# A convolution with generated weights and a two-branch maxout layer: columns taken in rotated order, a start with casting transfers, and row copies moved to VectorE

## The chip, the core and the metric

The kernel runs on one core of one Trainium2 chip. The metric is the device time of one execution in microseconds (us), the median of the runs. The core has a matrix engine (TensorE, PE in the profile; its loading of weights is PEld), VectorE (DVE), ScalarE (ACT), GpSimd (POOL) and SyncE (SP), and 16 DMA engines that move data between memory (DRAM) and the on-chip buffer (SBUF). SP and POOL are here above all issuers of transfers. A transfer that POOL issues may change the number format on its way (a casting transfer, f32 in DRAM to bf16 in SBUF); those that SP issues here copy as they are.

## The reference

x has 8 batches of 4160 rows of 192 numbers. Each row is replaced by a weighted sum of itself and its six predecessors in the same batch (zeros ahead of the first), with weights from a softmax over 7 taps for each of 8 heads of 24 numbers. The result y goes through h1 = y @ w1, h2 = y @ w2, g = max(h1, h2), out = g @ w_out:

```python
w = np.exp(weight_gen - max); w = w / (w.sum(-1) + 1e-09)      # 7 taps, 8 heads
x_pad = np.concatenate([zeros(B, 6, D), x], axis=1)
y[b, s, h] = sum over k of w[b, s, h, k] * x_pad[b, s + k, h]   # 24 numbers a head
g = np.maximum(y @ w1, y @ w2)                                  # (33280, 1024)
out = g @ w_out                                                 # (33280, 192)
```

The kernel uses max(h1, h2) = h1 + relu(h2 - h1): it computes y @ (w2 - w1), takes relu of it, and adds y @ (w1 @ w_out) in the second product.

## The kernel before, in words

The 33280 rows lie as 128 partitions of 260 columns: partition p holds rows 260p to 260p + 259, so 16 partitions make one batch of x. A column is one row of x in each partition. **Batches** (line 50) are runs of 16 columns for the softmax, 17 of them, the last of 4 columns. **Units** (line 63) are the pieces of a batch that VectorE turns into y: 4 columns in batches 0 and 1, 8 columns in the others, and the last batch is one unit of 4. **Tiles** (line 68) are pieces of hidden rows, 260 in all, one per column on average; **groups** (line 71) are two, later three, tiles.

For one unit, VectorE multiplies x by the weights (mul, L182, one instruction for all 7 taps) and adds the taps up (adds, L198, L204, L207). The result is turned round: by SP's DMA transpose (L216) from unit 8 on, by TensorE against an identity (sum_transpose, L248, with the adding done there too) and a ScalarE copy (L255) in units 0 to 7. TensorE then forms the hidden tile (hid_tile, L299), ScalarE takes its relu (L309), and TensorE adds the columns of the output (L351, L339), which ScalarE copies (L395) and SP stores (L409). For a batch's weights, ScalarE takes an exponential (exp_sum, L135), VectorE sums it (red, L147), ScalarE takes the logarithm (ln, L151), VectorE subtracts it (shift, L156), and ScalarE takes the exponential of that (weights, L167). The next loads are issued on POOL after an instruction `gate` that waits for a transpose's landing (L224).

Everything is issued in program order on each engine; there is no scheduler. The order after the start is given by `extra(t)` (line 758: which mul and adds go beside which tile) and by due times in `due` (line 731) for ScalarE's softmax steps. `behind(first, load)` makes a transfer wait until `first` is done.

**The start** (lines 520 to 695). SP issues, one behind another: the softmax input of batch 0 (wg_t); the six columns before column 0, the halo, which are the last six of the partition above (xs, L523, in two transfers); columns 0 to 3 (L532); the first halves of w1 and w2, rows 0 to 127 (ws0E, ws1E, L541); their rows 128 to 191, in four transfers (ws0T, ws1T, L549); columns 4 to 7; the second halves of w1 and w2 (L541 again); and the softmax input of batch 1. All of it is f32. In partitions that begin a batch the halo must be zero: a mask (L557 to L561) multiplies it (L568 on VectorE, L570 on ScalarE), while L574 and L620 cast columns 0 to 3 and 4 to 7 to bf16. VectorE's order is: softmax of batch 0, casts, mul of unit 0, `w_diff(0)` (the difference of the first halves L584 and of the last rows L589), cast L620, mul of unit 1, `w_diff(1)`, red of batch 1, mul of unit 2. The copies of difference rows to other partitions (L586, L587, L591) are on ScalarE in `w_diff(0)` and on VectorE in `w_diff(1)`. ScalarE casts w1 to bf16 (L580, L633, L634), which w1_transposed (L603) needs. TensorE's first matmuls are only there to keep it busy (keep_warm, L615): 30 ahead of the first sum_transpose and 8 behind it. Hidden tiles 0 and 1 use the first halves of the difference, 2 and 3 the second.

**The end.** The last batch is the unit of 4 columns; TensorE's last work is the output of the last 8 columns (rest_of_results, line 489).

## Time and profile before

| | |
|---|---|
| time, median of 3 runs (lowest, highest) | 410.28 us (409.76, 410.6) |
| span of the profiled execution | 408.8 us |
| between the span and the median | 1.5 us |
| busy: PE, DVE, ACT, POOL | 399.1, 373.4, 357.2, 75.5 us |
| first mul, first hidden tile start | 9.12, 15.47 us |
| last y on DVE ends, last hidden tile starts | 379.30, 397.22 us |
| last matmul ends | 404.98 us |

The trace gives the profiled execution's span, from its first to its last instruction; a time of that one execution with what lies around the span is not given, so the 1.5 us stand between its span and the median of the runs. A row of the timeline has the start, the duration, the engine, the line, the operation with what it writes and reads, the shape, the number of such instructions, and in brackets how long the engine was idle before it and what ended that. Durations of queued instructions overlap a little. "POOLq" and "SPq" rows are issues of transfers; the transfers land some us later.

### The profile page before, as it was taken

To read this page: it belongs to the slowest core of one execution; us is meant where nothing else is said; L and a number is where in the kernel's file an instruction comes from. 1 tells how busy PE (TensorE), PEld (TensorE's weight loads), DVE (VectorE), ACT (ScalarE), POOL (GpSimd) and SP (SyncE) were. 2 spreads that over 40 slices of the span, in tenths; PEclk is the share of its full clock that TensorE was granted. 3 is DMA by queue.
4 is the path that set the end of the run, shared out by engine and by line. 5 is a ranking of instruction groups with operands and counts; after the bars stand their busy time and mean duration, and the time that the engine had idled before them with its cause. 6 is when DMAs were issued, how large, how long until landed. Compare 5 with 4: busy or idle time off the path is not lost.

```text
span 408.8 us, 16064 instructions
## 1 busy us (share of the span) xinstructions
PE 399.1 (98%) x7386; PEld 317.5 (78%) x7386; DVE 373.4 (91%) x217; ACT 357.2 (87%) x424; POOL 75.5 (18%) x101
## 2 busy tenths in 40 slices
PE   7899999999999999999999999999999999999996
PEld 2688999777777877778777777877787776787796
DVE  5999999999999999999999999999999999999100
ACT  6799999999899998999998999998999888988872
POOL 0311011222221022221111222220121221210000
PEclk9999999999999999999999999999999999999999
DMA  8958477667647854965785397478649638643704
GB/s 240 229 118 217 126 148 164 159 150 182 148 102 198 226 129 98 260 167 85 214 231 117 91 256 186 74 243 168 146 98 250 169 59 223 177 88 108 187 35 161
DMA packets 60784, 65.68 MB, mean 161 GB/s; under 512 B 47631, under 2 KB 49039, under 8 KB 60718
## 3 DMA queue, kind: packets, MB, share of 16 engines
q1 hardware_dynamic: 52334, 40.54, 35.6%
q0 software_dynamic: 8240, 24.04, 29.5%
q8 instruction: 57, 0.93, 0.9%
q10 hardware_dynamic: 144, 0.10, 0.1%
q14 instruction: 9, 0.07, 0.1%
HBM read 35.96 MB, written 25.56 MB: 150 GB/s over the span
## 4 chain that ended last, share of the span: by engine, by line
PE 78%; DVE 7%; ACT 7%; DMA 5%; issue 1%; SPq 1%; DVEq 0%; ACTq 0%
PE op_ps L339 36%; PE hd L299 33%; PE op_ps L351 7%; ACT rd_t L309 4%; DVE m_t L182 4%; DMA ws1T<-in_moe_w_dram 2%; DMA out_dram<-o_t 1%; PE hdp L299 1%; PE yps L248 1%; DVE m_t L204 1%; DVE m_t L198 1%; DMA yt<-y_t 1%; ACT en_t L167 1%; ACT o_t L395 1%; DVE y_t L207 0%
## 5 line engine op out<-in xcount | busy, mean ns | idle before, releaser
L309 ACT ACTIVATE rd_t<-hd 128x1024 bf16<-128x1024 f32 (+1 forms) x206 | 234.4, 1188 | 27.8 <-PE hd L299 26.6
L339 PE MATMUL op_ps<-wo,rd_t 64*128 64x192 bf16 x4160 | 211.4, 243 | 0.4 <-issue 0.3
L339 PEld LDWEIGHTS <-rd_t 64*128 64x128 bf16 x4160 | 181.5, 94 | 16.2 <-issue 0.5
L299 PE MATMUL hd<-yt,wd 64*128 64x512 bf16 (+1 forms) x1584 | 187.8, 360 | 0.9 <-DMA yt<-y_t 0.7
L182 DVE TENSOR_TENSOR m_t<-xb_t,en_t 128x10752 bf16<-128x10752 bf16 (+1 forms) x37 | 187.4, 5070 | 0.2
L299 PEld LDWEIGHTS <-wd 64*128 64x128 bf16 x1776 | 94.8, 94 | 42.4 <-issue 2.0
L224 POOL CAST gate<-yt 128x1 f32<-128x1 bf16 x29 | 41.0, 1415 | 264.6 <-DMA yt<-y_t 264.6
L198 DVE TENSOR_TENSOR m_t<-m_t 128x4608 bf16<-128x4608 bf16 (+1 forms) x31 | 75.5, 2434 | 0.1
L395 ACT COPY o_t<-op_ps 128x384 f32<-128x384 f32 (+1 forms) x99 | 57.1, 588 | 13.4 <-PE op_ps L339 13.4
L351 PE MATMUL op_ps<-w,yt 64*128 64x192 bf16 x780 | 55.9, 243 | 0.2 <-ACT o_t L395 0.2
L351 PEld LDWEIGHTS <-yt 64*128 64x128 bf16 x780 | 38.5, 94 | 16.5 <-issue 1.3
L204 DVE TENSOR_TENSOR m_t<-m_t 128x3072 bf16<-128x3072 bf16 (+1 forms) x29 | 50.0, 1723 | 0.1
L167 ACT ACTIVATE en_t<-wg_t 128x896 bf16<-128x896 f32 (+2 forms) x45 | 35.6, 817 | 0.0
L207 DVE TENSOR_TENSOR y_t<-m_t 128x1536 bf16<-128x1536 bf16 (+1 forms) x29 | 27.3, 941 | 0.5
L114 POOL DMA_DIRECT2D xb_t<-in_x_dram x33 | 17.6, 534 | 29.9 <-ACT rd_t L309 18.9
L156 DVE TENSOR_TENSOR wg_t<-wg_t,sum_t 128x280 f32<-128x280 f32 (+5 forms) x46 | 22.0, 480 | 0.0
L147 DVE TENSOR_REDUCE sum_t<-e_t 128x64 f32<-128x448 f32 (+2 forms) x31 | 19.6, 635 | 2.6 <-ACT e_t L135 2.5
L135 ACT ACTIVATE e_t<-wg_t 128x896 f32<-128x896 f32 (+2 forms) x18 | 16.1, 901 | 2.5 <-DMA wg_t<-in_weight_gen_dram 2.5
L309 ACT ACTIVATE rd_t<-hdp 128x1024 bf16<-128x1024 f32 x16 | 16.2, 1031 | 0.6 <-PE hdp L299 0.4
L615 PE MATMUL warm<-ident 128*128 128x512 bf16 x38 | 11.5, 474 | 2.6 <-DVE ident L562 2.6
L299 PE MATMUL hdp<-yt,wd 64*128 64x256 bf16 x192 | 13.5, 270 | 0.3 <-issue 0.2
L248 PE MATMUL yps<-ident,m_t 64*128 64x64 bf16 x600 | 10.5, 191 | 1.5 <-DVE m_t L182 1.5
(45 smaller groups left out, 65.0 us busy)
## 6 DMA issues: line engine op xcount, KB each, us to landing
out_dram<-o_t SPq DMA_DIRECT2D x27, 768.0 KB, 4.9
xb_t<-in_x_dram POOLq DMA_DIRECT2D x30, 384.0 KB, 5.1
wg_t<-in_weight_gen_dram POOLq DMA_DIRECT2D x14, 448.0 KB, 5.4
xb_t<-xb_t POOLq DMA_DIRECT2D x16, 288.0 KB, 5.2
out_dram<-o_t SPq DMA_DIRECT2D x10, 384.0 KB, 3.3
wg_t<-in_weight_gen_dram SPq DMA_DIRECT2D x2, 448.0 KB, 4.5
xs<-in_x_dram SPq DMA_DIRECT2D x2, 384.0 KB, 6.7
xb_t<-in_x_dram POOLq DMA_DIRECT2D x3, 192.0 KB, 5.0
```

Of the source, the lines that this page charges most:

```text
L156: nc.vector.tensor_tensor(out=w_t, in0=w_t, in1=_sub(s_ts[b], hs.start, [[1, hs.stop - hs.start], [0, K]]), op=ALU.subtract)
L167: nc.scalar.activation(out=_sub(en_ts[b], (o * WGC + j * N * K) * 2, [[2 * N, K], [2, N], [1, 2]]), in_=_sub(wg_ts[b], (o * H + j * N) * K ...
L182: return nc.vector.tensor_tensor(out=m_out, in0=x_in, in1=_sub(en_ts[b], o * WGC * 2, [[2, K * n * H], [0, G // 2], [1, 2]]), op=ALU.mult,)
L198: nc.vector.tensor_tensor(out=taps(0, 1, 3), in0=taps(0, 1, 3), in1=taps(3, 1, 3), op=ALU.add)
L204: nc.vector.tensor_tensor(out=taps(0, 2, 2), in0=taps(0, 2, 2), in1=taps(1, 5, 2), op=ALU.add)
L207: nc.vector.tensor_tensor(out=_sub(y_ts[b], o * D, [[64, 2], [P, 3 * w // 2], [1, 64]]), in0=taps(0, 1, 1), in1=taps(2, 1, 1), op=ALU.add,)
L224: nc.gpsimd.tensor_copy(out=gate, in_=yt[:, 0:1])
L299: nc.tensor.matmul(hid_out(t, f, j), lhsT=wd_at(j, s, f // 4, f % 4 * P, P), rhs=_sub(yt_ts[u][half(j), :], (s + j) % 3 * P, [[3 * P, w // ...
L309: relu_of[t0] = nc.scalar.activation(out=rd[:, k * 1024:(k + n) * 1024], in_=hd[:, at:at + n * 1024], func=AF.Relu)
L339: return nc.tensor.matmul(op_out(c), lhsT=rd[half(r), k * 1024 + at:k * 1024 + at + P], rhs=wo[half(r), f * D:(f + 1) * D], start=False, s ...
L351: nc.tensor.matmul(op_out(c + j), lhsT=yt_ts[u][half(j), (3 * i + (s + j) % 3) * P:(3 * i + (s + j) % 3 + 1) * P], rhs=w10[half(j), s * D: ...
L395: nc.scalar.copy(out=_sub(o, c % 24 * D, [[D, len(qs)], [h * D, 2], [1, D]]), in_=_sub(tile_, at + (qs[0] - p) * D, [[D, len(qs)], [512, 2 ...
```

## The change

Columns are taken in an order rotated by 8: the kernel's column c is column (c + 8) mod 260 of the partition. The first batch is then columns 8 to 23, whose six predecessors are in the same partition, and the last batch is columns 0 to 7, whose halo is the end of the partition above. Batch 15 has 12 columns (units of 8 and 4), batch 16 has 8 (two units of 4).

At the start one casting transfer on POOL brings halo and first four columns of batch 0, ten columns; the mask and the four casts are gone, the halo of the last batch comes from DRAM with zeros copied over the partitions that begin a batch. SP's transfers of the weights wait for the first exponential. The last rows of w1 and w2 are issued half on SP, half on POOL. The second half of w1 comes a second time as a casting transfer, so L634 is gone. All copies of difference rows are on VectorE, and `w_diff(1)` stands ahead of the mul of unit 1. There are 19 and 5 matmuls of keep_warm. Hidden tile 2 and w1_transposed stand ahead of the sum_transpose of unit 1.

```diff
-    BATCHES = [(c, min(16, CPP - c)) for c in range(0, CPP, 16)]
+    ROT = 8
+    BATCHES = [(c, min(16, CPP - ROT - c)) for c in range(0, CPP - ROT, 16)] + [(CPP - ROT, ROT)]
+    def dcol(c):
+        return (c + ROT) % CPP
...
-        for w in (4, 4, 4, 4) if b < 2 else (8, 8) if n == 16 else (n,):
+        for w in (4, 4, 4, 4) if b < 2 else (8, 8) if n == 16 else (8, 4) if n == 12 else (4, 4):
...
         (load_halo)
-        nc.gpsimd.dma_start(out=xb_ts[b][:, 0:PAD * D],
-                            in_=xb_ts[b - 1][:, 16 * D:(16 + PAD) * D])
+        if b < NB - 1:
+            nc.gpsimd.dma_start(out=xb_ts[b][:, 0:PAD * D],
+                                in_=xb_ts[b - 1][:, 16 * D:(16 + PAD) * D])
+            return
+        nc.gpsimd.dma_start(
+            out=xb_ts[b][1:P, 0:PAD * D],
+            in_=bass.AP(tensor=x.tensor, offset=(CPP - PAD) * D, ap=[[CPP * D, P - 1], [1, PAD * D]]),
+        )
+        nc.gpsimd.dma_start(out=xb_ts[b][0:P:RPB, 0:PAD * D], in_=zeros[0:P:RPB, :])
...
         load_wg(0, nc.sync)
-        (xs: memset, halo in two transfers, load_first(0), load_w(0), last rows, load_first(4), load_w(1), load_wg(1))
-        (mask on POOL and DVE)
+        make_identity(nc, ident_f)
+        xb_ts[0] = pxb.tile([P, (16 + PAD) * D], BF16, name="xb_t", tag="xb")
+        nc.gpsimd.dma_start(
+            out=xb_ts[0][:, 0:(PAD + 4) * D],
+            in_=bass.AP(tensor=x.tensor, offset=(ROT - PAD) * D, ap=[[CPP * D, P], [1, (PAD + 4) * D]]),
+        )
+        nc.gpsimd.memset(zeros, 0.0)
...
+        first_exp = exp_sum(0, 0, 2)
+        exp_sum(0, 1, 2)
+        for step in (red, ln, shift):
+            for i in range(2):
+                step(0, i, 2)
+        behind(first_exp, load_w(0)[0])
+        for h, eng in enumerate((nc.sync, nc.gpsimd)):
             for wi, wsrc in enumerate((moe_w1, moe_w2)):
+                load = eng.dma_start(
                     out=ws["T", wi][half(h), :],
                     in_=bass.AP(tensor=wsrc.tensor, offset=P * F + h * HF, ap=[[F, 64], [1, HF]]),
                 )
+                if h:
+                    behind(first_exp, load)
         load_w(1)
         load_wg(1, nc.sync)
+        first_weights = weights(0, 0)
+        behind(first_weights, load_x(0, 4, 4))
+        for o in (4, 8, 12):
             weights(0, o)
         first_mul = mul(0, 0)
+        behind(first_mul, load_x(0, 8, 4))
+        nc.gpsimd.dma_start(
+            out=w1["E"][:, HF:F], in_=bass.AP(tensor=moe_w1.tensor, offset=HF, ap=[[F, P], [1, HF]]),
+        )
+        (the transfer of wo, load_x(0, 12, 4))
         nc.scalar.copy(out=w1["E"][:, 0:HF], in_=ws["E", 0][:, 0:HF])
+        nc.scalar.copy(out=w1["T"], in_=ws["T", 0])
-        keep_warm(30)
-        w_diff(0, nc.scalar.copy)
-        nc.vector.tensor_copy(out=xb_ts[0][:, (PAD + 4) * D:(PAD + 8) * D], in_=xs[:, (PAD + 4) * D:])
+        keep_warm(19)
+        w_diff(0, nc.vector.tensor_copy)
         sum_transpose(0)
-        keep_warm(8)
+        keep_warm(5)
+        w_diff(1, nc.vector.tensor_copy)
         mul(0, 4)
-        nc.scalar.copy(out=w1["E"][:, HF:F], in_=ws["E", 0][:, HF:F])
         (hidden tile 0, relu, exp_sum(1), hidden tile 1, relu)
-        w_diff(1, nc.vector.tensor_copy)
-        sum_transpose(1)
         red(1)
         mul(0, 8)
-        hidden(1)
+        rd = room(1)
+        hid_tile(2)
+        relu(rd, 2, 1)
+        tp = w1_transposed()
+        sum_transpose(1)
         ln(1)
         shift(1)
         mul(0, 12)
+        hid_tile(3)
+        relu(rd, 3, 1)
...
-        hidden(2)
         (copies of tp, weights(1, 0), mul(1, 0))
+        (hidden tiles 4 and 5 with their relu, w10_product, w10_copies)
         sum_transpose(2)
...
+        if 4 in dict(pieces(c)):
+            parts_.append((16 * (c - 2) + 18, True, lambda c=c: weights(c, 4)))
...
+        if s == 8 and b + 2 == NB:
+            mul(b + 1, 4)
+            adds(b + 1, 4)
```

In the diff, text in round brackets stands for lines that are told in words.

More of the change, by code (lines that the diff above doesn't have):

```diff
@@ L312, in column @@
     def column(c):
[L314 to L317 removed]
+        for u, (b, o, n) in enumerate(UNITS):
+            k = c - BATCHES[b][0] - o
+            if 0 <= k < n:
                 return u, k // 2, k % 2
@@ L677 @@
         mul(1, 0)
+        rd = room(2)
+        hid_tile(4)
+        relu(rd, 4, 1)
+        hid_tile(5)
+        relu(rd, 5, 1)
+        behind(relu_of[5], load_wg(2, nc.gpsimd))
+        pw = w10_product()
+        w10_copies(pw)
         sum_transpose(2)
```

88 lines of the change are left out of this document (21 added, 67 removed).

## The prediction

> **What bounds the kernel now.** I read the page's busy shares first. PE is busy 98% of the span and DVE 91%, and the row of DVE's slices is full until it stops near 380 us. So two engines are full at once, and the question for any edit is which of them passes its gain on to the end.
>
> ```profile
> span 408.8 us, 16064 instructions
> PE 399.1 (98%) x7386; PEld 317.5 (78%) x7386; DVE 373.4 (91%) x217; ACT 357.2 (87%) x424; POOL 75.5 (18%) x101
> DVE  5999999999999999999999999999999999999100
> L182 DVE TENSOR_TENSOR m_t<-xb_t,en_t 128x10752 bf16<-128x10752 bf16 (+1 forms) x37 | 187.4, 5070 | 0.2
> ```
>
> The last line says that in the whole run mul waited 0.2 us. DVE never pauses after the start; what shifts its start shifts all of it.
>
> The timeline then gives the pace of both. PE's hidden pairs start at 353.11, 361.75 and 370.38 us: 8.64 us per 6 tiles, 11.52 us per unit of 8. DVE's mul starts at 316.38, 328.24 and 340.05 us: 11.83 us per unit. DVE is slower by 0.3 us a unit and eats up the lead that it has early on. Near the end the lead is gone, and the waits show it:
>
> ```profile
> 340.05 5.75 DVE L182 TENSOR_TENSOR m_t<-xb_t,en_t 128x10752 bf16<-128x10752 bf16 x1
> 345.13 0.82 PE L299 MATMUL hd<-yt,wd 64*128 64x512 bf16 x6 [0.71 <-DMA yt<-y_t]
> ```
>
> This is unit 32 (batch 14, first half). It is PE's only wait for a transpose. After it, DVE's softmax steps get shorter (batch 16 has 4 columns), so the lead grows again: y of the last unit lands at about 383.8 us (the gate's start) and its first tile starts at 391.21. So the end is the later of two chains: **PE's own**, which without that wait would end at 408.8 - 0.7 = 408.1, and **DVE's up to unit 32**, which gives 408.8. A gain g_PE in the first and g_D in the second move the end by the smaller of (g_PE + 0.7) and g_D.
>
> Now the start, where the change is. The timeline of the first 25 us:
>
> ```profile
> 4.51 1.04 ACT L135 ACTIVATE e_t<-wg_t 128x448 f32<-128x448 f32 x2 [2.49 <-DMA wg_t<-in_weight_gen_dram]
> 8.45 0.56 DVE L574 CAST xb_t<-xs 128x768 bf16<-128x768 f32 x1 [0.83 <-DMA xs<-in_x_dram]
> 9.12 2.96 DVE L182 TENSOR_TENSOR m_t<-xb_t,en_t 128x5376 bf16<-128x5376 bf16 x1
> ...
> 13.19 0.69 DVE L589 TENSOR_TENSOR wd<-ws1T,ws0T 128x512 bf16<-128x512 f32 x1 [0.51 <-DMA ws1T<-in_moe_w_dram]
> 13.89 0.96 DVE L620 CAST xb_t<-xs 128x768 bf16<-128x768 f32 x1
> 14.96 2.96 DVE L182 TENSOR_TENSOR m_t<-xb_t,en_t 128x5376 bf16<-128x5376 bf16 x1
> ...
> 17.98 1.40 PE L248 MATMUL yps<-ident,m_t 64*128 64x64 bf16 x84 [1.02 <-DVE m_t L182]
> 19.42 0.80 ACT L255 CAST yt<-yps 128x768 bf16<-128x768 f32 x1 [0.28 <-PE yps L248]
> 20.43 2.95 DVE L182 TENSOR_TENSOR m_t<-xb_t,en_t 128x5376 bf16<-128x5376 bf16 x1
> ```
>
> Three transfers set it: x (8.45), the last weight rows (13.19), then the mul of unit 1 at 14.96, which PE (17.98) and ACT (19.42) wait for. The DMA engines' share of the windows of half a microsecond is 0.9 to 1.2 from 2.5 to 20 us: they are full, and what lands when is a matter of bytes and order.
>
> **Part 1, first product.** L568, L574, the mask and DVE's wait of 0.83 us go; ACT loses L570 (1.02). The weights are then ready as follows: the first half of shift ends at 6.8, and two L167 of some 0.31 us (8 take 2.45) with their latency of 0.4 give 7.5. The ten columns: POOL is free at 1.5, a casting load of 8 columns lands 5.1 us after issue (median of 30; 5.4 in the emptiest stretch, issued at 28.05). Two columns more are 0.20 MB at 0.346 MB/us, 0.6 us: landing at 7.2 to 7.5. The 0.346: that load and a plain one of 0.46 MB fill 3.8 us of the engines from 29 to 33.5, the plain one alone takes 1.53 us (25 to 27.5), so 0.786 MB of source takes 2.27 us. First mul at 7.5 instead of 9.12, **1.6 us earlier**. Bounds: 7.5 by the weights; 8.5 if x lands as late as today.
>
> **Part 2, weights and their differences.** DVE then has mul 2.96, w_diff(0) with its copies (0.69 + 0.29 + 0.29 + 0.69 + 0.33, the copies from DVE's rows at 18.56, where they cost 0.29 against ACT's 0.62), 2.3: free at 12.8, against 14.96 today, since L620 (0.96) goes too. But now w_diff(1) stands ahead of the mul of unit 1, and it needs the second halves of w1 and w2. Today those are issued at 8.44 and 9.73 and land 6.1 and 5.4 us later, at 14.5 and 15.1. Call their landing E; **all else hangs on it**.
>
> ```profile
> ws1E<-in_moe_w_dram SPq DMA_DIRECT2D x1, 256.0 KB, 5.4
> xs<-in_x_dram SPq DMA_DIRECT2D x1, 384.0 KB, 6.3
> ```
>
> By bytes: today columns 0 to 3 land at 2.08 + 6.3 = 8.4, and from there to 15.1 the engines deliver first halves, last rows, four columns and second halves, 1.97 MB in 6.7 us, 0.293 MB/us. After the change the same set follows x from about 7.4, with the four columns cast (0.39 x 0.87 = 0.34): 1.91 MB, 6.5 us, E = 13.9. To this comes what POOL's later loads (x of unit 2, the second copy of w1's half, wo), issued at 10.5 behind the first product instead of 12.4, take from the same engines: nothing, or an equal share from 11.7 on, some 0.3 MB, 1 us. So 13.9 to 14.9; the wider ends are 13.0 (today's shortest issue-to-landing 5.4, from an issue at 7.6) and 15.8 (the longest, 8.1). SP's wait for the first exponential (5.0) costs nothing if the engines are busy with x until about 6.2. I take **E = 14.2**, a third of the equal share, since SP's transfers are ahead of POOL's in time.
>
> Splitting the last rows over SP and POOL I count as the issue time alone, 1.2 us on SP. The Trainium skill, page "DMA: Bandwidth & Descriptors", section "Issuing engines are not separate DMA queues", says the same: all queues run on the same 16 engines, a second issuer saves only issue time. By that rule E stays near 14; without it two queues would move more, and the second rival below would be the outcome. No row of this trace has both queues moving weights.
>
> **What follows from E.** DVE: 0.05 + w_diff(1) 1.6 (17.84 to 19.40 today) + mul 2.96 + red 1.04 (19.43 to 20.43), so unit 2's mul starts at E + 5.65 = 19.85, against 20.43: **g_D = 0.6**. Up to unit 32 batch 15's shorter softmax adds to it: red of 6 instead of 8 columns (448 elements cost 0.61 and 112 0.26, so 336 cost 0.50), 2 x 0.12, and shift of 4, 4, 4 instead of 5, 5, 6 columns (0.44, 0.44, 0.50 to 0.385 each), 0.23: together 0.5. DVE's side gives 1.1.
>
> PE and ACT: the sum_transpose of unit 1 starts at E + 4.65 = 18.85, against 17.98, 0.9 later. But one hidden tile (0.75) and w1_transposed (0.9) are done ahead of it now, and one relu (0.97) ahead of ACT's copy of it. PE gains 1.65 - 0.9 = 0.8, ACT 0.97 - 0.9 = 0.1. ACT has hardly a gap from 12.7 to 32 us today, so I take nearer its end: **g_PE = 0.3**, and with the 0.7 of the vanished wait 1.0. The casts L633 and L634 (0.62 each) stood ahead of the first relu and are covered now by ACT's wait for unit 1.
>
> **Part 3, the middle and the end.** The middle is untouched. In the end 12 hidden tiles have chunks of 256 instead of 4: two such tiles take 1.49 us against 1.48, nothing. Three units of 4 replace one of 8 and one of 4: DVE +0.6 (2 x (2.95 + 2.87) against 5.75 + 5.25). POOL issues x, halo and zeros of the last batch from about 357, zeros only after the halo has landed: by two landings of 5.2 us, 368; mul of it can't start before ACT's weights (368.7 to 369.3 today) either, where DVE would be free at 367. These 2 us and the 0.6 are covered by the 7 us between the last landing (383.8) and its use (391.2). Uncovered they would cost 1:1. The output's last stores keep their sizes.
>
> **Sum.** min(1.0, 1.1) = 1.0 us off a span of 408.8. With the same 1.5 us around it, 410.28 - 1.0 = **409.3**.
>
> **Rivals.** (1) *The gain is hidden by the same bytes*: E between 14.6 and 15.9. Then g_PE + 0.7 = 15.2 - E lies between +0.6 and -0.7: about 410.2. For it: the byte sum is nearly unchanged, and POOL's loads start sooner. (2) *No wait for the second halves*: E up to 13.4, towards 12.8. DVE runs through, 1.6 to 2.0 us gained: 408.4. For it: all seven SP issues are out by 8.4, where SP today waits for landings before it issues the second halves. (3) *Slower, one mechanism*: w_diff(1) at DVE's head of the queue blocks mul of unit 1, red, mul of unit 2, and PE and ACT behind them. Every us of E costs one; from E = 15.2 nothing is left, from 16.0 it is slower by over 0.8 us; at 16.7, 411.8. Against it: no weight transfer of today took over 8.1 us, which gives 15.8. (4) *PE loses its clock* in the longer gap ahead of unit 1's sum_transpose: the first 14 keep_warm matmuls run at 0.43 us, the others at 0.216; a second such ramp would cost up to 3 us, 412. Today's gap of 1.0 us at 17 us does nothing; mine are 1.5 us at most.
>
> The Trainium skill, "TensorE: Matmul & The Clock Gate", section "Why this matters for your kernels", puts the harmful gap at about 3 us; by that rule (4) needs E above 16.
>
> **Chances.** Forecast (E 13.4 to 14.6, 408.7 to 409.7) 0.42; (1) 0.24; (2) 0.20; (3) 0.11; (4) 0.03. A difference below 0.2% (0.82 us) can't be told from none here. Two thirds of the forecast's case and all of (2) are beyond that: faster 0.50; same 0.35; slower 0.15. Range: from all of (2), 408.1, to the lower part of (3), 411.2.
>
> **What would show it.** Right: first mul near 7.5; DVE's L584 waiting for the second halves near 14; unit 2's mul near 19.9; no wait for yt, or a small one, near 344; last y near 379. Wrong: x landing after 8.5, a wait of DVE past 15, a wait for yt in the last three units, or keep_warm's 0.43 us returning.

## The result and the profile after

The changed kernel takes **412.02 us** (median of 20 runs, 410.84 to 413.92), the kernel before 410.73 us in the same comparison (20 runs). The ratio is 1.0035, with a 95% interval from 1.0022 to 1.0047: slower by about 1.4 us, where 1.0 us less was forecast. The profiled execution took 411.65 us with a span of 409.5, 0.7 us over the span of before. It is a short one of its kind (median of the 20 spans: 409.85), and 2.15 us lie around the spans of the changed kernel against 1.8 to 2.0 around those of the kernel before (medians, the latter beside the later runs). So the two single profiles show about half of the loss, and a comparison of medians is needed for its size.

The page after, its lines that answer to those of before:

```profile
span 409.5 us, 16139 instructions
...
PE 397.1 (97%) x7420; PEld 319.0 (78%) x7420; DVE 372.4 (91%) x217; ACT 353.9 (86%) x420; POOL 77.3 (19%) x108
...
DVE  3899999999999999999999999999999999999300
...
L195 DVE TENSOR_TENSOR m_t<-xb_t,en_t 128x10752 bf16<-128x10752 bf16 (+1 forms) x38 | 187.7, 4941 | 2.7 <-DMA xb_t<-in_x_dram 1.9
```

Still two full engines, each with a little less work than before (PE 397.1 against 399.1, which has 14 warm matmuls more; DVE 372.4 against 373.4). But mul's idle time is 2.7 us instead of 0.2, of which 1.9 us lie ahead of one mul and end with x. DVE's row begins with 38 where before had 59: the loss is in the first two slices, 20 us.

Near unit 32, where PE waited 0.71 us before, the timeline shows:

```profile
341.33 5.75 DVE L195 TENSOR_TENSOR m_t<-xb_t,en_t 128x10752 bf16<-128x10752 bf16 x1
...
345.28 1.48 PE L312 MATMUL hd<-yt,wd 64*128 64x512 bf16 x12
```

No wait for yt is left; 12 matmuls run through. PE's own chain sets the end now, and it started late.

The rows of the timeline that carry the start (in brackets the idle time before the row):

```profile
6.33 2.46 ACT L179 ACTIVATE en_t<-wg_t 128x224 bf16<-128x224 f32 x8 [0.27 <-DVE wg_t L168]
...
8.70 2.96 DVE L195 TENSOR_TENSOR m_t<-xb_t,en_t 128x5376 bf16<-128x5376 bf16 x1 [1.87 <-DMA xb_t<-in_x_dram]
...
11.72 1.46 PE L261 MATMUL yps<-ident,m_t 64*128 64x64 bf16 x84 [3.63 <-DVE m_t L195]
...
12.43 0.69 DVE L586 TENSOR_TENSOR wd<-ws1E,ws0E 128x512 bf16<-128x512 f32 x1 [0.77 <-DMA ws1E<-in_moe_w_dram]
...
13.11 2.31 PE L617 MATMUL warm<-ident 128*128 128x512 bf16 x5
...
13.45 0.59 DVE L589 COPY wd<-wd 64x512 bf16<-64x512 bf16 x1
...
15.99 0.69 DVE L586 TENSOR_TENSOR wd<-ws1E,ws0E 128x512 bf16<-128x512 f32 x1 [0.90 <-DMA ws1E<-in_moe_w_dram]
...
17.55 2.96 DVE L195 TENSOR_TENSOR m_t<-xb_t,en_t 128x5376 bf16<-128x5376 bf16 x1
...
20.56 1.40 PE L261 MATMUL yps<-ident,m_t 64*128 64x64 bf16 x84 [0.32 <-DVE m_t L195]
...
21.42 2.95 DVE L195 TENSOR_TENSOR m_t<-xb_t,en_t 128x5376 bf16<-128x5376 bf16 x1
...
34.34 0.82 PE L312 MATMUL hdp<-yt,wd 64*128 64x256 bf16 x12
```

DVE waits three times for a transfer: x (1.87), the first halves (0.77), the second halves (0.90). The mul of unit 1 starts at 17.55 instead of 14.96, that of unit 2 at 21.42 instead of 20.43, and tile 8, the first of the steady part, at 34.34 instead of 32.28.

The landings behind these waits (casting load of x; second half of w2), and the DMA engines while x is on its way (the last two columns of the stretches are the share of the 16 engines and GB/s, the one ahead of them the granted clock):

```profile
xb_t<-in_x_dram POOLq DMA_DIRECT2D x1, 480.0 KB, 7.2
ws1E<-in_moe_w_dram SPq DMA_DIRECT2D x1, 256.0 KB, 8.1
```
```profile
3.50:4.50 1.00, 1.00 (x4) 0.30 (x2) 0.00 (x0) 0.49 (x2) 0.00 (x0) 1.00 0.63 123
...
5.50:6.50 1.00, 1.00 (x5) 0.42 (x4) 1.00 (x3) 0.46 (x3) 0.47 (x1) 1.00 0.72 85
6.50:7.50 1.00, 1.00 (x7) 0.41 (x6) 0.33 (x1) 1.00 (x4) 0.17 (x1) 1.00 0.61 124
...
13.00:16.00 3.00, 3.00 (x21) 1.07 (x17) 1.99 (x6) 1.32 (x2) 1.47 (x3) 0.50 1.09 312
```

x was issued at 1.42 and landed at 8.6. Before SP's first weight goes out (at 4.61, against 2.55 before) the engines were 63% busy: the casting load does not fill them, and the weights that could have used the rest were held back for it. From 5.5 to 7.5 us, with the first weights issued, they were still at 72 and 61%; why is not shown. The last line shows a second loss: the granted clock is 0.50 from 13 to 16 us, after the gap of 3.63 us.

### The profile page after: what moved, and what is told of

The parts are those of the page before. It is cut to its first block, busy times and chain, and to the rows that moved or that the text cites. A ratio compares the mean times of both kernels' runs of the same rounds, so it can differ in the third digit from the quotient of the medians.

```text
span 409.5 us, 16139 instructions
## 1 busy us (share of the span) xinstructions
PE 397.1 (97%) x7420; PEld 319.0 (78%) x7420; DVE 372.4 (91%) x217; ACT 353.9 (86%) x420; POOL 77.3 (19%) x108
## 4 chain that ended last, share of the span: by engine, by line
PE 85%; ACT 8%; DMA 3%; DVE 2%; issue 1%; SPq 1%; ACTq 0%; DVEq 0%
PE op_ps L351 39%; PE hd L312 38%; PE op_ps L363 7%; ACT rd_t L322 4%; DMA ws1E<-in_moe_w_dram 2%; ACT en_t L179 1%; DVE m_t L195 1%; DMA wg_t<-in_weight_gen_dram 1%; ACT o_t L407 1%; ACT yt L268 1%; ACT e_t L147 1%; SPq L544 0%; PE hdp L312 0%; SPq L557 0%; DVE sum_t L159 0%
## 5 line engine op out<-in xcount | busy, mean ns | idle before, releaser
L312 PEld LDWEIGHTS <-wd 64*128 64x128 bf16 x1824 | 96.7, 94 | 42.3 <-issue 2.3
L237 POOL CAST gate<-yt 128x1 f32<-128x1 bf16 x30 | 38.2, 1275 | 266.4 <-DMA yt<-y_t 266.4
L363 PEld LDWEIGHTS <-yt 64*128 64x128 bf16 x780 | 38.3, 94 | 15.9 <-issue 1.3
L168 DVE TENSOR_TENSOR wg_t<-wg_t,sum_t 128x280 f32<-128x280 f32 (+6 forms) x46 | 22.0, 481 | 0.4 <-ACT sum_t L163 0.2
L159 DVE TENSOR_REDUCE sum_t<-e_t 128x64 f32<-128x448 f32 (+3 forms) x31 | 19.6, 634 | 3.1 <-ACT e_t L147 3.1
L322 ACT ACTIVATE rd_t<-hdp 128x1024 bf16<-128x1024 f32 x16 | 15.9, 1038 | 2.5 <-PE hdp L312 2.5
L261 PEld LDWEIGHTS <-m_t 64*128 64x128 bf16 x600 | 9.7, 95 | 5.3 <-DVE m_t L195 4.6
```

Source lines behind the costliest of these rows:

```text
L168: nc.vector.tensor_tensor(out=w_t, in0=w_t, in1=_sub(s_ts[b], hs.start, [[1, hs.stop - hs.start], [0, K]]), op=ALU.subtract)
L237: nc.gpsimd.tensor_copy(out=gate, in_=yt[:, 0:1])
L312: nc.tensor.matmul(hid_out(t, f, j), lhsT=wd_at(j, s, f // 4, f % 4 * P, P), rhs=_sub(yt_ts[u][half(j), :], (s + j) % 3 * P, [[3 * P, w // ...
L322: relu_of[t0] = nc.scalar.activation(out=rd[:, k * 1024:(k + n) * 1024], in_=hd[:, at:at + n * 1024], func=AF.Relu)
L363: nc.tensor.matmul(op_out(c + j), lhsT=yt_ts[u][half(j), (3 * i + (s + j) % 3) * P:(3 * i + (s + j) % 3 + 1) * P], rhs=w10[half(j), s * D: ...
```

## The experiments

Each kernel was compared with the kernel before in runs on one chip. Three theories stood at first. **L**: the weights land late, everything behind their differences follows. **C**: the clock that PE loses in the gap of 3.63 us is the price. **R**: the rotated columns with the new end cost something of their own. The runs of e and g, of h, of i1, h5, h6 and g1 again, and of j1 were on four different chips, so across these groups the ratios are compared. Edits are against the changed kernel in e1 to g4 (g1: against the kernel before), against "rotation alone" (g1) from h1 on (j1: against i1). A start of tile 8 is given for each, since PE runs nearly without a pause from there on; the pauses that it still has (0.4 us in all in the changed kernel, 1.4 in the kernel before) blur this.

| kernel | median us (before) | ratio, 95% interval | mul of unit 1, of unit 2, tile 8 |
|---|---|---|---|
| changed kernel | 412.02 (410.73) | 1.0035 [1.0022, 1.0047] | 17.55, 21.42, 34.34 |
| e1 differences behind mul | 411.70 (410.14) | 1.0042 [1.0020, 1.0064] | 15.77, 21.20, 33.44 |
| e2 30 warm matmuls | 412.59 (410.14) | 1.0048 [1.0023, 1.0072] | 17.51, 21.39, 34.98 |
| e3 weights at once | 411.04 (410.14) | 1.0027 [1.0008, 1.0046] | 16.75, 21.08, 33.82 |
| e4 half of w1 loaded once | 413.26 (410.14) | 1.0067 [1.0041, 1.0092] | 16.82, 20.69, 35.52 |
| g1 rotation alone | 408.61 (410.23) | 0.9962 [0.9936, 0.9987] | 12.71, 18.14, 30.58 |
| g2 e2 and e3 together | 411.98 (410.23) | 1.0035 [1.0009, 1.0061] | 17.60, 21.47, 33.96 |
| g3 x as f32 on SP | 409.78 (410.23) | 0.9981 [0.9956, 1.0005] | 17.18, 21.05, 33.33 |
| g4 reordered start | 410.40 (410.23) | 1.0002 [0.9978, 1.0026] | 14.95, 20.41, 32.65 |
| h1 g1 + last rows on two queues | 412.56 (410.32) | 1.0044 [1.0030, 1.0059] | 15.22, 20.65, 33.79 |
| h2 g1 + casting load | 411.43 (410.32) | 1.0018 [0.9994, 1.0042] | 14.63, 20.06, 32.48 |
| h3 g1 + differences ahead | 410.71 (410.32) | 1.0008 [0.9991, 1.0025] | 15.56, 19.43, 32.43 |
| h4 g1 + copies on DVE | 409.94 (410.32) | 0.9990 [0.9976, 1.0004] | 14.12, 19.54, 31.35 |
| i1 h1 without its wait | 410.03 (410.14) | 0.9991 [0.9969, 1.0013] | 13.56, 18.99, 31.81 |
| h5 g1 + halo as 16 and 112 | 409.91 (410.14) | 1.0001 [0.9976, 1.0026] | 14.14, 19.57, 31.69 |
| h6 g1 + halo as 1, 15, 112 | 410.19 (410.14) | 0.9999 [0.9975, 1.0024] | 13.56, 19.04, 31.50 |
| g1 again | 408.50 (410.14) | 0.9951 [0.9930, 0.9972] | 12.84, 18.26, 30.44 |
| j1 i1, later loads held | 411.09 (410.76) | 1.0007 [0.9984, 1.0031] | 14.30, 19.75, 32.29 |

**e1: the differences behind the mul of unit 1**, and tile 2 and w1_transposed behind its sum_transpose, as before.

```diff
         keep_warm(5)
-        w_diff(1, nc.vector.tensor_copy)
         mul(0, 4)
...
+        w_diff(1, nc.vector.tensor_copy)
+        sum_transpose(1)
...
-        sum_transpose(1)
```

> The changed kernel with w_diff(1) moved behind the mul of unit 1 on VectorE, and hidden tile 2 and w1_transposed moved behind the sum_transpose of unit 1 on TensorE, as they stood in the kernel before. Theory L (late second halves): in the trace of the change VectorE stands 0.90 us for the second halves (landing 15.95) and then 1.6 us in w_diff(1) while the mul of unit 1 could have begun when x of unit 1 landed (7.33 + 8.4 = 15.7). So that mul starts near 15.8 instead of 17.55 and the sum_transpose of unit 1 near 18.8 instead of 20.56; the mul of unit 2 stays near 21.4, since the same work only changes places. PE and ACT gain 1.8 less one relu (0.97) that falls back behind unit 1, 0.85 us; VectorE's chain to unit 32 stays 0.5 us behind that of before and shows as a wait for yt near 344. Time 0.5 us under the change, 0.5 to 0.8 over before. Theory C (clock): the loss is TensorE at half clock from 13.0 to 16.4 us; the gap ahead of the first sum_transpose is unchanged, so no change. Theory R (the rotated end costs): no change.

The mul of unit 1 starts 1.78 us earlier, but now it waits 0.34 us for columns 4 to 7, and unit 2's mul starts at 21.20: 0.2 us gained. Tile 8 starts 0.9 us earlier, but this lead is down to 0.3 us by 57 us (two short pauses of PE for which the profile names no releaser) and to 0.1 near the end. The ratio can't be told from the changed kernel's. So the head of DVE's queue is not all of it: the whole series of landings is late, and another order only changes which of them DVE meets.

**e2: 30 warm matmuls instead of 19**, so that PE has no long gap ahead of its first sum_transpose.

```diff
-        keep_warm(19)
+        keep_warm(30)
```

> The changed kernel with 30 keep_warm matmuls at first instead of 19, so that TensorE is busy until the first sum_transpose (11 more at 0.216 us: from 8.1 to 10.5, a gap of 1.2 us instead of 3.6). Theory C: the granted clock stays 1.00, the first two hidden tiles take 1.49 us instead of 1.94 and the time falls by the whole loss, 1.3 us. Theory L: the clock stays 1.00 too, the first relu comes 0.5 us earlier, but unit 1's mul still starts at 17.5 us and everything from there is unchanged: time within 0.3 us of the change. Theory R: no change.

The gap ahead of the first sum_transpose is 1.16 us, the granted clock 1.00 from 7 to 19 us, and unit 2's mul starts where it did (21.39). The clock then falls from 19 to 23 us (0.63 on average; the sum_transpose at 20.55 takes 2.44 us). The time is not better. C alone is not the cause: with the clock kept up to 19 us, the late landings remain. e1 shows the same more plainly: there the granted clock is 1.00 from 7 to 24 us, and the time is still that of the changed kernel.

**e3: SP's weights at once.**

```diff
-        behind(first_exp, load_w(0)[0])
+        load_w(0)
```

> The changed kernel without the wait of SP's weight transfers for the first exponential: they are issued from 1.2 us on instead of 4.6. Theory L: in the trace of the change the 16 DMA engines are only 34 to 99% busy between 3.5 and 8 us (mean 75%), 1.1 us of their time, since the casting load alone doesn't fill them. Without the wait they are full, the second halves land at 13.5 to 14.5 instead of 15.95, x of the first product lands up to 1 us later than 8.55. The mul of unit 1 starts near 16.4 instead of 17.55, the time falls by 1.1 us, to about that of before. Theory C: the gap of TensorE grows by what x is later; no gain. Theory R: no gain. If the casting load is slowed by much more than 1 us, the first product is late and the time rises.

x now lands at 9.2 instead of 8.6. The engines' share is 0.98 to 1.11 in the stretches from 3.5 to 7.5 us, and they have moved 1.83 MB by 8.6 us instead of 1.29. The second half of w2, issued at 4.21, lands at 13.2 instead of 15.9, but VectorE is not yet there: POOL's halves of the last rows, still issued behind the first exponential (5.42 and 5.96), land 7.5 and 8.1 us later, at 12.9 and 14.1, and the difference of the last rows starts behind them. The landing, and the row of VectorE:

```profile
ws1E<-in_moe_w_dram SPq DMA_DIRECT2D x1, 256.0 KB, 9.0
```
```profile
14.10 0.69 DVE L591 TENSOR_TENSOR wd<-ws1T,ws0T 128x512 bf16<-128x512 f32 x1 [0.64 <-issue]
```

So the second difference starts at 15.20 instead of 15.99, without a wait of its own, and tile 8 is 0.5 us earlier; the ratio can't be told from the changed kernel's. L's direction is right: the wait for the first exponential alone put off the second halves by 2.7 us, but without it x is 0.6 us later and the last rows become what VectorE waits for. The clock falls here as well (0.66, 0.50 and 0.70 in the stretches from 10 to 19 us).

**e4: the second half of w1 is loaded once** and cast by ScalarE, here behind the relu of tile 2.

```diff
-        nc.gpsimd.dma_start(
-            out=w1["E"][:, HF:F], in_=bass.AP(tensor=moe_w1.tensor, offset=HF, ap=[[F, P], [1, HF]]),
-        )
...
+        nc.scalar.copy(out=w1["E"][:, HF:F], in_=ws["E", 0][:, HF:F])
```

> The changed kernel without the second, casting transfer of w1's second half; ScalarE casts it from the f32 copy as in the kernel before (0.62 us, ahead of w1_transposed). Theory L: 0.26 MB less on the engines at 13 to 16 us; the second halves land up to 0.4 us earlier and the wait of w1_transposed for that transfer (0.69 us) goes, which is not on the path, as the sum_transpose of unit 1 waits for VectorE. Time 0.3 us under the change. If the second copy of w1's half were the whole reason for the late landing, the second halves would land at 14.9 and the time fall by 1 us. Theories C and R: no change.

The second difference starts at 15.27, 0.7 us earlier. That this is engine time which POOL's second copy took is not shown: the first halves are as much earlier in this execution (the last lands at 11.6, not 12.3), ahead of the copy's issue (12.49 in the changed kernel). And w1_transposed stands ahead of the sum_transpose and waits 2.0 us for ScalarE's cast; tile 8 is 1.2 us later. The second copy is worth its bytes in that order of work.

**g1: the rotation alone.** The start of the kernel before (f32 loads on SP in its order, engine casts, 30 and 8 warm matmuls, differences behind the mul), with rotated columns, the new last batch, and the halo in one transfer of 128 partitions without a mask.

```diff
-        (halo in transfers of 15 and 112 partitions, memset, mask)
+        nc.sync.dma_start(
+            out=xs[:, 0:PAD * D],
+            in_=bass.AP(tensor=x.tensor, offset=(ROT - PAD) * D, ap=[[CPP * D, P], [1, PAD * D]]),
+        )
```

> The kernel before with the rotated column order and its end (12 and 8 columns, three units of 4, halo of the last batch from DRAM), and nothing else of the change: the start is that of before, x in f32 on SP, without the mask. Theory R (the rotation or its end costs the time): 1.3 us over before. Theories L and C: the end is covered by the lead behind unit 32, and batch 15's shorter softmax gives VectorE 0.5 us up to unit 32, so the wait for yt near 344 is 0.2 us instead of 0.7: between 0.7 us under before and equal to it.

It is **faster than both kernels**: 408.61 us here, 408.50 when measured again. That is more than L and C had allowed (0 to 0.7 us). R falls: the new end costs nothing, and all of the loss is in the start. Two rows from its first timeline, with nothing in brackets:

```profile
7.92 2.96 DVE L195 TENSOR_TENSOR m_t<-xb_t,en_t 128x5376 bf16<-128x5376 bf16 x1
...
12.71 2.96 DVE L195 TENSOR_TENSOR m_t<-xb_t,en_t 128x5376 bf16<-128x5376 bf16 x1
```

x and last rows are there when DVE comes to them. The same two rows have 9.12 and 14.96 before, 8.70 and 17.55 after.

**g2: e2 and e3 together.**

```diff
-        behind(first_exp, load_w(0)[0])
+        load_w(0)
...
-        keep_warm(19)
+        keep_warm(30)
```

> The changed kernel with SP's weights issued at once (as in e3) and 30 keep_warm matmuls. In e3's trace TensorE lost its clock from 12.3 to 17 us, its first two hidden tiles ended 1 us late and the sum_transpose of unit 1 stood behind them at 20.70, 1 us after VectorE's product was there (19.7). Theory L with the clock as a second, smaller cause: that sum_transpose starts at 19.75, tile 8 near 33 instead of 33.82, the time falls by 0.7 to 1.0 us against e3, to about that of before. If the clock counts for nothing: as e3 (0.9 over before).

The ratio is the changed kernel's. x landed at 10.6, 1.4 us later than in e3 with the same transfers; that eats what the weights gain, and PE has a gap of 3.09 us all the same. When the casting load shares the engines, its landing is not only late but uncertain: 9.2, 10.6, and 9.7 in h2.

**g3: the ten columns as f32 on SP** and cast by engines, weights at once, the rest as changed.

```diff
-        nc.gpsimd.dma_start(
-            out=xb_ts[0][:, 0:(PAD + 4) * D],
+        for c0, c1 in ((0, PAD), (PAD, PAD + 4)):
+            nc.sync.dma_start(
+                out=xs[:, c0 * D:c1 * D],
...
-        behind(first_exp, load_w(0)[0])
+        load_w(0)
```

> The changed kernel with the ten columns brought as f32 by SP in two transfers (halo, four columns) and cast by VectorE and ScalarE as in the kernel before; the weights follow on SP at once. The question is what the casting load does. In the trace of the change it took 7.15 us for 0.98 MB with the engines 75% busy. If the casting load is what is slow: x lands at 8.4, the first mul starts at 9.1 (with its cast), the second halves land 0.5 to 1 us before e3's 15.1, and the time is 0.5 us under e3's. If casting and plain loads move the same bytes in the same time: x and second halves as in e3, the casts cost VectorE 0.9 us, the time is 0 to 0.9 us over e3's.

The first mul starts at 7.82 without a wait for x. The last rows are late now: POOL's half, still behind the first exponential, lands at 13.4 and 14.5, and DVE idles 2.57 us ahead of the difference. The time is 2.2 us below the changed kernel's and 1.2 us above g1's: the second culprit has a name.

**g4: reordered start.** Weights at once and all on SP, last rows too; columns 4 to 7 right behind the first ten; e1's order; 30 warm matmuls; the casting load stays.

```diff
+        load_x(0, 4, 4)
...
-        behind(first_exp, load_w(0)[0])
-        for h, eng in enumerate((nc.sync, nc.gpsimd)):
+        load_w(0)
+        for h, eng in enumerate((nc.sync, nc.sync)):
...
-        keep_warm(19)
+        keep_warm(30)
-        w_diff(1, nc.vector.tensor_copy)
```

> An attempt at a better order from what theory L says: the changed kernel with all weights on SP at once, all last rows on SP, columns 4 to 7 issued by POOL right behind the first ten, w_diff(1) behind the mul of unit 1 (hidden tile 2 and w1_transposed behind its sum_transpose), 30 keep_warm matmuls. First mul near 9.2, last rows land near 13, the mul of unit 1 starts near 14.4 (before: 14.96), that of unit 2 near 20.0 (before: 20.43), the sum_transpose of unit 1 near 17.5 (before: 17.98). PE gains 0.5 and VectorE 0.4 + 0.5 at unit 32 over before: 0.9 us under before. If the casting loads of x take the engines from the last rows, these land at 14 and the time is that of before.

No different from the kernel before: with most other parts undone, the gain of the rotation is gone. The casting load (x at 9.5) is the largest part left; the copies on VectorE and the second copy of w1 are still there too, and the granted clock is 0.50 from 13 to 15 us.

**h1 to h4: one part of the change each, on top of g1.**

```diff
h1:
-        for wi, wsrc in enumerate((moe_w1, moe_w2)):
-            for h in range(2):
-                nc.sync.dma_start(
+        for h, eng in enumerate((nc.sync, nc.gpsimd)):
+            for wi, wsrc in enumerate((moe_w1, moe_w2)):
+                load = eng.dma_start(
...
+                if h:
+                    behind(first_exp[0], load)
h2:
-        (ten columns in two f32 transfers on SP, casts by engines)
+        nc.gpsimd.dma_start(
+            out=xb_ts[0][:, 0:(PAD + 4) * D],
h3:
+        w_diff(1, nc.vector.tensor_copy)
         mul(0, 4)
...
-        w_diff(1, nc.vector.tensor_copy)
-        sum_transpose(1)
h4:
-        w_diff(0, nc.scalar.copy)
+        w_diff(0, nc.vector.tensor_copy)
```

> The kernel with the rotation alone (g1: 408.61 us, mul of unit 1 at 12.71 us, hidden tile 8 at 30.58) plus one part of the change: the second halves of the last weight rows are issued on POOL behind the first exponential, not on SP. Theory A (the parts of the start that stand beside the rotation each put off the weights, and this one does): POOL's two transfers of 64 partitions by 512 columns land 8 us or more after issue, as in the full change and in g3 (13.4 to 14.5), against 11.3 in g1; the difference of the last rows waits for them, mul of unit 1 starts at 14 to 15 and tile 8 at 31.5 to 32.5: 409.5 to 410.5. Theory B (two queues only save issue time): landing by 11.5, mul of unit 1 within 0.3 of 12.71, 408.3 to 408.9.

> g1 plus one part of the change: the ten columns of x by one casting transfer on POOL, so the casts on VectorE and ScalarE are gone; SP's weights are not held back. Theory A (a casting transfer is slower for what is needed first): x lands at 8.5 to 9.2 as in the full change and in e3, first mul 8.6 to 9.3 against 7.92, everything behind it 0.7 to 1.3 later, tile 8 at 31.2 to 32: 409.2 to 410. Theory B (its landing does not matter, the weights' does): first mul later, but mul of unit 1 and tile 8 within 0.3 of g1's, since VectorE saves casts: 408.3 to 408.9.

> g1 plus one part of the change: w_diff(1) ahead of mul of unit 1, hidden tile 2 and w1_transposed ahead of its sum_transpose. In g1 the second halves land at about 13.4 and VectorE is free at 12.71. Theory A (head of the queue blocks): VectorE waits 0.7 for the second halves, then 1.6 of w_diff(1) ahead of mul: mul of unit 1 at 15.0 to 15.3, unit 2's mul 0.7 later than in g1 (18.14), the sum_transpose of unit 1 at 18 to 18.6 with two tiles' worth of work done ahead of it: tile 8 within -0.3 to +1 of 30.58, 408.3 to 409.6. Theory B (the clock gate is what costs): TensorE's gap ahead of that sum_transpose grows to over 3 us, the granted clock drops to 0.5 and 1.5 to 2 us are lost: 410 or more.

> g1 plus one part of the change: the row copies of the first difference on VectorE, not on ScalarE. VectorE gets 3 copies of 0.29 to 0.33 us more ahead of mul of unit 1, ScalarE loses 3 of 0.62 ahead of its copy of unit 0's y. Theory A (each part of the start costs a little): mul of unit 1 0.9 later at 13.6, tile 8 0 to 0.9 later: 408.6 to 409.5. Theory B (this part gains, ScalarE being the later of the two): hidden tile 0 up to 1 us earlier, tile 8 0.3 to 0.9 earlier: 407.7 to 408.4.

All four are slower than g1, as theory A has it, and all four by more than A's range: the mul of unit 1 starts at 15.22, 14.63, 15.56 and 14.12, the times are 412.56, 411.43, 410.71 and 409.94. The rows that say why, from the timelines of h1, h2 and h3:

```profile
13.95 0.69 DVE L595 TENSOR_TENSOR wd<-ws1T,ws0T 128x512 bf16<-128x512 f32 x1 [2.59 <-DMA ws1T<-in_moe_w_dram]
```
```profile
9.81 2.96 DVE L195 TENSOR_TENSOR m_t<-xb_t,en_t 128x5376 bf16<-128x5376 bf16 x1 [2.71 <-DMA xb_t<-in_x_dram]
```
```profile
14.01 0.69 DVE L587 TENSOR_TENSOR wd<-ws1E,ws0E 128x512 bf16<-128x512 f32 x1 [0.39 <-DMA ws1E<-in_moe_w_dram]
...
15.56 2.96 DVE L195 TENSOR_TENSOR m_t<-xb_t,en_t 128x5376 bf16<-128x5376 bf16 x1
```

Each part puts a wait, or copies, ahead of the mul of unit 1 (in h4 three copies, of 0.29, 0.29 and 0.64 us; POOL issues transfers beside all three). With g1 at 0.9951 and 0.9962, taken as 0.9956, the ratios are higher by 0.0088, 0.0062, 0.0052 and 0.0034: about 3.6, 2.5, 2.1 and 1.4 us, each uncertain by about 1 us. Their sum, 9.6 us, is three times what the whole change loses against g1 (0.0079, 3.2 us). They don't add. All of them put off the same mul, so a wait for one can hide the wait for another; this is argued, as no run has all four on g1. h3's profiled execution (span 410.7) is a long one: the median of its spans is 408.85. The clock stayed at 1.00 in h3, where no gap of PE behind its first matmul is over 0.8 us, so its cost is not C's.

**g1 again**, with **i1: h1 without its wait**, **h5 and h6: the halo split**.

```diff
i1:
-                load = eng.dma_start(
+                eng.dma_start(
...
-                if h:
-                    behind(first_exp[0], load)
h5 (h6: (0, 1), (1, 16), (16, P)):
+        for p0, p1 in ((0, 16), (16, P)):
+            nc.sync.dma_start(
+                out=xs[p0:p1, 0:PAD * D],
```

> The rotation alone once more, as the measure for the three beside it and for h1 to h4: the same start (mul of unit 1 at 12.7, tile 8 at 30.6) and again faster than the kernel before, 408.2 to 409.4 (ratio 0.994 to 0.998), if the first result holds; a ratio at or over 0.999 would say that the 1.6 us were chance.

> h1 without the wait: POOL issues the second halves of the last rows right after its own first instructions (at about 2.3 us), not behind the first exponential (5.07). Theory T (what lands when follows the time of issue, and the wait is what cost h1 its 3 us): they land by 11, mul of unit 1 starts at 12.0 to 12.8 as in g1 (12.71), tile 8 within 0.5 of 30.58: 408.2 to 409.2. Theory Q (a transfer from POOL's queue is late in itself, whenever issued): difference of the last rows after 12, mul of unit 1 after 13.3, 409.5 or more.

> g1 with its halo of 128 partitions in two transfers, 16 and 112 partitions, as the kernel before loads it in 15 and 112. Theory S (the split of the halo is what slows the engines at the start of the kernel before, 230 to 300 GB/s at a share near 1 against 400 to 430, and so is most of what the rotation gains): rates near 300 from 4 to 6 us, x 0.5 to 1 us later, last rows at 12 to 13, mul of unit 1 at 13.5 to 14.5: 409.3 to 410.3. Rival (the gain is the mask and casts that are gone from VectorE): rates near 400, mul of unit 1 within 0.3 of 12.71, 408.3 to 409.

> g1 with its halo in three transfers, 1, 15 and 112 partitions: the 15 and 112 of the kernel before, and one more for the partition that needs none there. Theory S as for 16 and 112, with the odd count of 15 besides: if 15 is what slows the engines, this one shows the low rates (230 to 300 GB/s from 4 to 6 us) and 16 with 112 does not; mul of unit 1 then at 13.5 to 14.5, 409.3 to 410.5. Rival: only the issue time of two more transfers, 0.9 us on SP, which moves the last rows by as much: mul of unit 1 at most 0.9 later, 408.6 to 409.5.

g1's gain repeats. **h5 and h6** give back 1.4 and 1.7 us of its 1.6 (by the ratios, 2.0 of 2.0): theory S. The stretches of g1 again, then of h5:

```profile
4.00:5.00 1.00, 1.00 (x4) 0.33 (x3) 0.24 (x1) 0.85 (x2) 0.00 (x0) 1.00 1.02 419
5.00:6.00 1.00, 1.00 (x6) 0.45 (x5) 1.00 (x3) 0.51 (x3) 0.00 (x0) 1.00 1.03 345
```
```profile
4.00:5.00 1.00, 1.00 (x4) 0.32 (x3) 0.00 (x0) 0.24 (x1) 0.00 (x0) 1.00 0.94 249
5.00:6.00 1.00, 1.00 (x5) 0.42 (x4) 0.63 (x2) 0.80 (x2) 0.00 (x0) 1.00 1.04 240
```

The engines are about as full in both, and move 419 and 345 GB/s in the one, 249 and 240 in the other (244 and 284 in h6). A halo of the same bytes, cut into 16 and 112 partitions, makes the first microseconds slower; DVE's first exponential sum comes 0.6 us later, the first mul 1.25 us. Since 16 and 112 do it as well as 1, 15 and 112, an odd count of partitions is not the reason. One transfer more on SP takes 0.45 us of issue, which is a part of it. It is not all: the softmax input wg_t is issued ahead of the halo, at 0.74 in both, and lands 3.4 us after its issue in g1 again, 4.0 in h5 (3.8 in h6 and in the kernel before):

```profile
wg_t<-in_weight_gen_dram SPq DMA_DIRECT2D x1, 448.0 KB, 3.4
```
```profile
wg_t<-in_weight_gen_dram SPq DMA_DIRECT2D x1, 448.0 KB, 4.0
```

No issue time of a later transfer can do that. Why the split slows the engines stays open.

**i1** has the numbers that theory Q named, but not its reason. The wait itself was worth 1.7 us of the mul of unit 1 (15.22 with it, 13.56 without), but 0.7 us of that mul, and 1.5 us of the time, stay against g1 again. POOL's halves land first, at 8.6 and 10.7; SP's own land last, at 11.3 and 12.2:

```profile
12.29 0.69 DVE L593 TENSOR_TENSOR wd<-ws1T,ws0T 128x512 bf16<-128x512 f32 x1 [0.88 <-DMA ws1T<-in_moe_w_dram]
```

So POOL's queue is not late in itself. With two transfers fewer to issue, SP sends columns 4 to 7 and the second halves 1.2 to 2.4 us sooner (4.44 to 5.58, against 5.65 to 7.99), which led to the next theory: these take the engines from the last rows.

**j1: i1 with those later loads held** behind the softmax's subtraction.

```diff
-        load_first(4)
-        load_w(1)
-        load_wg(1, nc.sync)
...
+                first_shift = step(0, i, 2)
+        behind(first_shift, load_first(4))
+        load_w(1)
+        load_wg(1, nc.sync)
```

> i1 with SP's later transfers (columns 4 to 7 and the second halves, issued at 4.44 to 5.58 there) held behind the softmax's subtraction, which ends near 7.0, so that they go out at about 7 to 8, as in g1 (5.65 to 7.99). Theory P (saved issue time brings the transfers needed later into the engines together with the last rows, which get a smaller part of them): the last rows land by 11.4, the wait of 0.88 us ahead of their difference goes, mul of unit 1 starts at 12.6 to 12.9 against 13.56, tile 8 at 30.4 to 31.1: 408.2 to 409.2. Theory Q (two queues slow the last rows whatever follows): the wait stays at 0.6 or more, mul of unit 1 at 13.3 or later, 409.5 or more.

```profile
12.98 0.69 DVE L593 TENSOR_TENSOR wd<-ws1T,ws0T 128x512 bf16<-128x512 f32 x1 [1.09 <-DMA ws1T<-in_moe_w_dram]
```

Theory P falls: the later loads go out at 7.20 to 8.09, and the last rows land later still, at 12.9. The engines are full (0.99 to 1.11 from 6 to 12 us) but move only 181 to 268 GB/s. As Q has it, the split on two queues makes the last rows late whatever follows; by what mechanism stays open.

## Why the prediction was wrong, step by step

- **What bounds the kernel**: right. Two full engines, the end set by the later of two chains, and the middle unmoved. The wait for yt at unit 32 went, as forecast.
- **Part 1, the first mul at 7.5**: wrong, 8.70. The weights were ready (exponentials from 6.33), x was not: 7.2 us for the casting load where 5.7 to 6.0 were worked out from steady loads of the middle. By the rates of the trace the ten columns should have cost 0.6 us more than eight columns; at the start it was 2.1 us over the median of 5.1.
- **Part 2, the landing time E: the step that failed.** 14.2 was taken, with 15.8 as the wide end; the second halves landed at 15.9, and the second difference starts right behind them at 15.99. Two terms of the sum were mis-sized. The set of weights was let follow x "from about 7.4"; x landed 1.2 us later. And from there to E the engines moved 253 GB/s, where 0.293 MB/us was put: an estimated 1 us more, of which a part may be in the count, as a casting load is counted by the bf16 that it writes (480 KB for the ten columns). A third term was put at nothing: "SP's wait costs nothing if the engines are busy with x until about 6.2" was a condition that didn't hold. Their share was 0.61 to 0.94 in the stretches from 3.5 to 7.5, and without the wait the second halves land at 13.2 (e3) or 14.0 (g2, the same transfers), 1.9 to 2.7 us earlier. The premise "they are full, and what lands when is a matter of bytes and order" fails on the windows of before itself: a share of 1.11 goes with 449 GB/s there (3.0 to 3.5 us) and 0.96 with 104 (20.0 to 20.5). Splitting the last rows, counted as issue time alone, was wrong in sign: by itself it costs about 3.6 us on g1 (h1), of which about 1.5 stay without the wait for the exponential (i1).
- **What follows from E**: right in mechanism and size. Unit 2's mul was put at E + 5.65 and came at 15.99 + 5.43; the sum_transpose of unit 1 at E + 4.65, and came at + 4.57. PE's own lag, 1.45 us by the sum, is 2.06 at tile 8 and 1.5 at 58 us. "The gain turns into a loss from E = 15.2" gives +0.75 us for E = 15.95; the spans differ by +0.7. The medians of the times differ by 1.3 us: the profile of after is 0.35 us short of its kind, and some 0.2 us lie around the span.
- **Which rival it was**: by E on the border of the first (E up to 15.9) and the third (w_diff(1) at the head of DVE's queue, from 16.0), at the price that both name there. All three signs of being wrong that concern the start showed: x landed after 8.5, DVE waited past 15, and the 5 warm matmuls took 0.46 us each. e1 corrects the third rival's reason: with w_diff(1) out of the way the time is the same, since other landings are as late. Its mechanism is real (h3: 2.1 us on g1), but it is one of four, and none of them is *the* cause.
- **The fourth rival, the clock**, was given 0.03 and did not happen where it was put, but elsewhere. The gap ahead of unit 1's sum_transpose was 0.32 us. The gap ahead of the first sum_transpose, unit 0's, was 3.63, not "1.5 us at most", because 19 warm matmuls end at 8.09 and x was late; the granted clock was 0.50 from 13.0 to 16.2 us. It cost 0.45 us in the first two hidden tiles (1.94 against 1.49), yet e1, with the clock at 1.00 throughout, is no faster.
- **Part 3**: right. The tail shows DVE waits of 0.2 and 0.4 us for ScalarE's weights, all covered, and g1 carries the same end and is the fastest.
- **What was missed**: the rotation itself. Its halo in one transfer was not given a price; it is worth 1.4 to 2.0 us (h5, h6), and the parts beside it spend that and 1.4 us more.

The Trainium skill, "DMA: Bandwidth & Descriptors", section "Issuing engines are not separate DMA queues", says that a second issuer saves only issue time. h1, i1 and j1 agree that it brings no bandwidth, but differ in the rest: the split made the last rows later by 0.8 us or more without any wait (i1: 12.2 against at most 11.36 in g1 again), which no saving of issue time explains. The measurement decides. Section "Why a DMA increments its semaphore by 16 and not by 1" of the same page gives the engines that a transfer uses from its partitions: 16 for 128 as for 112 and 16. So by that rule h5 uses as many engines as g1; the rates of 249 against 419 GB/s, and the later landing of wg_t, have another reason, which no run here shows.

## What to carry to other kernels

In a start that is full of transfers, ask of each edit when the first thing that the bound engine needs will land, and don't take a landing time from the steady part of the trace: measure it with everything that is in flight beside it. A transfer that is held back "for free" is free only if the engines are full without it, so read their share in the stretch in question. And when a change is a bundle, run its parts one by one on top of the one that works: here one part gains 1.6 us and four others, which each looked harmless, take twice that.

## What the runs showed of the hardware

- With the casting load of x in flight and no weight issued yet, the engines' share was 0.63 (changed kernel, 3.5 to 4.5 us), and its ten columns took 7.2 us; two plain f32 loads of the same columns, with 1 MB of weights issued behind them by 5.6 us (g1 again), landed 4.4 and 5.1 us after issue.
- The engines at a share of about 1.0 moved between 181 GB/s (j1, 11 to 12 us) and 428 (i1, 3 to 4 us). "Full" says nothing of bytes.
- The clock's drop doesn't follow from the length of one gap. Gaps ahead of the first sum_transpose and the clock after them: 3.63 us (after) 0.50; 4.35 (e4), 3.47 (e3), 3.09 (g2), 2.68 (g3) and 2.56 (g4) 0.50 as well; but 3.57 (e1) and 3.05 (h2) 1.00. The Trainium skill, "TensorE: Matmul & The Clock Gate", section "Why this matters for your kernels", puts the harmful gap at about 3 us; the gap after agrees, e1, h2, g3 and g4 don't, so it is no sharp bound here.
- Of two DVE copies of the same shape that ran while POOL issued the transfer of wo, one took 0.29 us and the next 0.59 (13.15 and 13.45, changed kernel). So the longer one has not been shown to come from POOL's issuing.
- Between the span and the time lie 2.15 us in the changed kernel and 1.81 in g1 (medians): up to 0.3 us of the loss is in no instruction. It is 2.12 to 2.15 in the changed kernel, e1, e2, e3 and g2, and 1.78 to 1.84 in all other kernels of the table (medians). Its cause was not looked for.
